# GFNet mixing and SiLU block: the last inverse stage with the tables as weights, rows r and 94 - r folded, sixteen array tiles at once

## The chip, the cores and the metric

The kernel runs on one core of a Trainium2 chip. The metric is device time in microseconds of one launch. A profiled execution also has a span, from the first to the last instruction.

## The reference, cut to what matters

Per batch of 3008 tokens and 256 channels a real Fourier transform over the tokens is multiplied by a filter and transformed back. The result goes, as 24064 tokens, through a two-layer block with SiLU.

```python
X = np.fft.rfft(x, axis=1)                   # x: (8, 3008, 256)
F = (filt_r + 1j * filt_i)[None, :, :]
y = np.fft.irfft(X * F, n=3008, axis=1)
h = y.reshape(24064, 256) @ w_in             # w_in: (256, 2048)
g = h * (1.0 / (1.0 + np.exp(-h)))
out = g @ w_out                              # w_out: (2048, 256)
```

x and the filters are float32; w_in and w_out arrive as float64, and the kernel turns their bits into float32 at its start.

## The kernel before

**The dense block sets the beat.** It runs in 384 steps. A step takes one pair of token blocks (256 or 240 columns) and one pair of 128-wide pieces of the 2048 hidden channels, by a Strassen-like scheme: seven products in `hidden` (line L957, banks px and pyz), and seven in `project` (L1020, four banks acc, a0 to a3) for the step before. ScalarE copies px to abc and applies SiLU, VectorE adds the pyz halves and combines g (L928). A float32 product is two matmul records. A step has eight rounds: in each, `hidden` advances by one product, then `project` by one. In a step in `opened`, two products of `project` come first and none in rounds 0 and 2. In a step in `joined` the first products of a new pair go to banks a0 and a1 before a2.

**The transform is put in between.** 48 steps (six pairs) belong to one batch; I call them a frame and number them 0 to 47. While the steps of batch b run, the transform of batch b + 1 is finished and that of b + 2 begun. `put(step, round, piece, ...)` says after which round of which step a piece is issued; `at = 48 * b`, so `at - 10` is step 38 of the frame before. The engines' queues are in order: a piece waits for what is issued ahead of it. The pieces for batches 2 to 7, with their steps in a frame:

- `reverse_x` (16) copies x with its rows reversed to DRAM (xr); `load_fold` (23, 33, 41) brings x and xr to x_all, 8 DMAs on SP; `fold` (28 to 30, 36 to 38, 44 to 46) adds and subtracts them on VectorE (L499); `stage1_fold` (32, 40, 0) is the first forward stage (L509): 16 products of 24 rows, 32 columns and 512 moving columns, one in each 32x32 tile of the array; `evict_fold` (ScalarE) and `pairs_fold` (VectorE, stores by POOL) empty its banks.
- `load_x`, `sums`, `stage1` (1 to 4) do the two leftover columns of the first stage.
- `load_t2`, `forward_two` (8, 16, 24), `free_two`, `multiply_two`, `add_two` (9 to 12 for the first) do the second forward stage and the filter.
- `inverse_two` (16, 24, 32), `even_two`, `rows_two`, `ends_two` do the first inverse stage and write d2 in DRAM.
- `load_t4`, `stage3` and `evict_y` are the last inverse stage, in eight groups of four positions. A group is 32 products (L742): the data (48 rows by 64 channels) are the weights, a table of 47 columns is the moving operand, channels come out on partitions. Its two banks are copied to y (L764), one by VectorE and one by ScalarE, 376 columns each. The groups stand in steps 37/38 (0 and 1, alone at the opening), 40 (2 and 3), 0 (4), 8 (5) and 11/12 (6 and 7); in the last frame in 0, 8, 11 and 16.

Batch 0 is transformed ahead of the first step, which begins at 75.25 us, in its own way (four of its last groups stand in steps 10 to 18), and batch 1 with other forward pieces; its last stage stands like that of the others.

`tokens` forms the sums ty of a pair on VectorE (L928), at (6,1), (11,5), (22,5), (26,6), (38,1) and (46,1), given as step and round. Stores of the result and all loads above are issued by SP. A wait at the head of its queue holds what is behind.

PSUM has eight banks: px and pyz (called HIDDEN), a0 to a3 (ACCS are a2 and a3) and two spare ones. A piece's `home` says which it takes; a bank of HIDDEN must be empty again before the next step's products.

Of the kernel before, what the change touches and what calls it, by code (L numbers as in the profile page):

```python
# [79 lines left out]

def rows_of(blocks):

    out = np.empty((B, NR, 2, 16, 4, 2, 32), np.float32)
    for (b, half, c0, n), block in zip(token_pairs(), blocks):
        for k in range(4):
            r0 = (c0 + n * (k // 2)) // 16
            out[b, r0:r0 + n // 16, half, :, :, OUT_HALF[k]] = (
                block[k, :, 0:n].reshape(4, 32, n // 16, 16).transpose(2, 3, 0, 1))
    return out.reshape(B * S, C)
# [100 lines left out]
def folded_tables():  # L190
# [14 lines left out]
    wn = np.zeros((128, 2, N1))  # L205
    for g in range(NG):
        for bank in range(2):
            for j in range(4):
# [7 lines left out]
                if j % 2 == 0:  # L216
                    row = 16 * (g // 2) + 4 * j + 4 * (g % 2) + 2 * bank
                    for h in range(2):
                        ph = 2 * np.pi * ((2 * np.arange(N1) + h) * s % 94) / 94
                        for half in range(2):  # L220
                            wn[64 * h + row, half] = 2 * np.cos(ph) / S if s else 1.0 / S
                            wn[64 * h + row + 1, half] = (2 * half - 1) * 2 * np.sin(ph) / S if s else 0.0
    f32 = np.float32
    return d.reshape(128, NS * 32).astype(f32), e.reshape(128, NG * 128).astype(f32), wn.astype(f32)
# [3 lines left out]
def kernel(  # L228
# [24 lines left out]
    dn_host, en_host, wn_host = folded_tables()  # L253
    dn_dram = nc.inline_tensor(dn_host, name="dn_tbl")
    en_dram = nc.inline_tensor(en_host, name="en_tbl")
    wn_dram = nc.inline_tensor(wn_host, name="wn_tbl")
# [28 lines left out]
    wn_t = cpool.tile([128, 2, N1], FP32)  # L285
# [29 lines left out]
    y = {}  # L315
# [18 lines left out]
    def spectral(b):  # L334
# [151 lines left out]
        def fold(f, k):  # L486

            used = slice(0, 120)
            if k == 0:
                us["f"] = upool.tile([128, 2, 512], FP32, name=f"uf_{b}_{f}", tag="u")  # L490
# [10 lines left out]
        def stage1_fold(f):  # L501
            ut = us.pop("f")
            rhs = x_all[:, 0, 0], x_all[:, 1, 0], ut[:, 0], ut[:, 1]
            home = (*HIDDEN, *ACCS) if f == 0 else (0, 1, None, None)
# [200 lines left out]
        def rows(g, i, n=1):  # L705
# [6 lines left out]
            for a in range(n):  # L712
                a0 = 8 * (g + a) + 4 * i
                nc.gpsimd.dma_start(out=d2[a0:a0 + 4].rearrange("a n h c -> (a n) h c"), in_=qt[:, a])
# [13 lines left out]
        def stage3(g, home=None):  # L728

            half, n0 = divmod(4 * g, 16)  # L730
            back = b > 1 and half
            table = wn_t[:, half] if b > 1 else wi_t
# [3 lines left out]
            t4 = us["t4"][:, 4 * g:4 * g + 4] if b == 0 and g < 4 else t4s[g]  # L736
            for cb in range(2):
                for i in range(4):
                    for c0 in (0, 64):
                        for h in range(2):  # L740
                            rows = slice(64 * h, 64 * h + 2 * NS)
                            nc.tensor.matmul(  # L742
                                out=ps[h][c0:c0 + 64, cb, 3 - i if back else i, :],
                                lhsT=t4[rows, i, 128 * cb + c0:128 * cb + c0 + 64],
                                rhs=table[rows, :], start=True, stop=True)
            if g < 6 and (b > 0 or g > 3):
# [11 lines left out]
        def evict_y(g, h):  # L758
            half, n0 = divmod(4 * g, 16)
            if b > 1 and half:  # L760
                n0 = 12 - n0
# [3 lines left out]

        return dict(us=us, store_rows=store_rows, evict_y=evict_y, pairs_t1=pairs_t1, halves=halves, load_first=load_first, stage1_first=stage1_first, fill_first=fill_first, load_x=load_x, load_two=load_two, sums=sums, stage1=stage1, reverse_x=reverse_x,
                    load_fold=load_fold, fold=fold, stage1_fold=stage1_fold, evict_fold=evict_fold, pairs_fold=pairs_fold, forward_two=forward_two, free_two=free_two, multiply_two=multiply_two, add_two=add_two, inverse_two=inverse_two, even_two=even_two, rows_two=rows_two, ends_two=ends_two,
                    load_t2=load_t2, forward=forward, multiply=multiply, add=add, inverse=inverse, inverse_first=inverse_first, rows_first=rows_first, even=even, rows=rows, load_t4=load_t4, load_t4_rows=load_t4_rows, stage3=stage3)
# [12 lines left out]
    def plan(b, part):  # L781
# [6 lines left out]
        else:  # L788
            put(at - 80, 0, part["reverse_x"])
            for f, step, load, places, ends in (  # L790
                    (0, -64, -73, ((-68, 3), (-68, 5), (-67, 5), (-66, 5)), ((1, 0), (1, 3))),
                    (1, -56, -63, ((-60, 3), (-60, 5), (-59, 5), (-58, 5)), ((1, 3), (1, 5))),
                    (2, -48, -55, ((-52, 3), (-52, 5), (-51, 5), (-50, 5)), ((1, 3), (1, 5)))):
# [7 lines left out]
            opened.add(at - 63)  # L801
# [30 lines left out]
        put(at - 14, 5, part["load_t4"], 0)  # L832
        put(at - 14, 5, part["load_t4"], 1)
        open_step(at - 10, *alone(part, 0), (part["stage3"], 1))
        put(at - 10, 3, part["evict_y"], 1, 0)
        put(at - 10, 5, part["evict_y"], 1, 1)
        join(at - 8, part, 2, 3)
# [12 lines left out]
    def plan_two(b, part):  # L850
# [18 lines left out]
        put(at - 12, 1, part["load_t4"], 0)  # L869
        put(at - 12, 1, part["load_t4"], 1)  # L870
        two_alone(at - 10, part, 0)
        join(at - 8, part, 2, 3)
        plan_rest(b, part)

    def two_alone(step, part, g):

        open_step(step, *alone(part, g), (part["stage3"], g + 1))
        put(step, 3, part["evict_y"], g + 1, 0)
        put(step, 5, part["evict_y"], g + 1, 1)
# [25 lines left out]
    def plan_rest(b, part):  # L905
# [6 lines left out]
        else:  # L912
            join(at, part, 4)
            join(at + 8, part, 5)
            if b == B - 1:
                alone_at(at + 11, 3, part, 6)
                join(at + 16, part, 7)
            else:
                two_alone(at + 12, part, 6)
# [178 lines left out]
    def load_weights(j, queue=None):  # L1098
# [4 lines left out]
        else:  # L1103
# [18 lines left out]
            in_=moe_w_in.bitcast(U32)[:, 256 * j:256 * j + 256].rearrange("(a p) n -> p a n", p=128))  # L1122
# [322 lines left out]
```

## Time and profile before

| | before |
|---|---|
| device time, median of 3 runs | 2573.54 us (2571.95 to 2575.02) |
| profiled execution, device time | 2574.01 us |
| its span | 2571.5 us |
| granted TensorE clock, mean | 0.996 |
| last stage's matmuls (L742, batches 2 to 7): busy, records | 52.8 us, 3072 |
| its weight loads | 48.5 us, 3072 |
| its copies to y (L764): VectorE, ScalarE | 32.9 us x60, 28.5 us x60 |
| first fold stage's matmuls (L509), two rows | 21.3 + 20.3 us, 576 |
| waits of pyz for VectorE's g (PEld, PE) | 27.7 us, 10.5 us |

Ends of matmuls are modelled and the matmuls are pipelined, so that a busy share of TensorE is not its share of the peak. A row of a group reads: line, engine, operation, out<-in, shapes, count, then busy us and mean ns of one, then the engine's idle time before it with what ended it. A row of the timeline reads: start us, us, engine, line, operation, out<-in, count, and in brackets the idle time before it.

### The profile page before, as it was taken

Reading aid. Unit: us, or ns where it says so; the run is one execution under the profiler, and the core shown is the slowest. Engines: PE = TensorE matmul, PEld = TensorE weight load, DVE = VectorE, ACT = ScalarE, POOL = GpSimd, SP = SyncE. Lnnn points to the kernel's source line nnn. Section 1 sums busy time; section 2 is a strip of 40 time slices with the busy share of each in tenths; the row PEclk is TensorE's granted clock in tenths of the full one; section 3 lists DMA queues with packets and bytes.
Section 4 is the critical chain, followed back from the end, with each engine's and each line's share of the span. In section 5 each row is a group of like instructions: output and inputs, shape, how many; then the busy total and the mean of one; then the engine's idle time right before and its main releaser. Section 6 shows DMA issues by size and latency. Waiting matters only on the chain.

```text
span 2571.5 us, 47151 instructions
## 1 busy us (share of the span) xinstructions
PE 2531.8 (98%) x18810; PEld 2183.9 (85%) x18810; DVE 1660.8 (65%) x3451; ACT 1103.6 (43%) x3039; POOL 438.5 (17%) x682
## 2 busy tenths in 40 slices
PE   8999999999999999999999999999999999999998
PEld 6688788888888888888888888888888888888987
DVE  7866656577666776667766676666766666554544
ACT  3544344444444444444444444444444444444443
POOL 3211111022111111211121111211121111101101
PEclk9999999999999999999999999999999999999999
DMA  9622142222322222331324203332042211200000
GB/s 288 163 69 78 39 111 59 65 62 65 72 68 69 58 69 59 85 83 35 75 55 97 72 25 75 83 78 63 25 98 61 60 42 33 62 15 16 16 9 17
DMA packets 122740, 171.84 MB, mean 67 GB/s; under 512 B 20500, under 2 KB 96244, under 8 KB 121636
## 3 DMA queue, kind: packets, MB, share of 16 engines
q1 hardware_dynamic: 97352, 117.88, 18.0%
q0 software_dynamic: 22320, 45.80, 6.7%
q10 hardware_dynamic: 2848, 5.15, 0.7%
q8 instruction: 147, 2.41, 0.4%
q14 instruction: 73, 0.60, 0.1%
HBM read 96.91 MB, written 81.26 MB: 69 GB/s over the span
## 4 chain that ended last, share of the span: by engine, by line
PE 93%; DVE 3%; DMA 3%; ACT 1%; issue 0%; SPq 0%; ACTq 0%; POOL 0%; POOLq 0%; DVEq 0%
PE acc L1020 43%; PE px L957 25%; PE pyz L957 19%; PE pd L742 3%; PE pc L604 1%; PE pb L566 1%; DVE g L928 1%; PE pf L509 1%; DVE q L616 1%; PE pa L420 0%; DMA filt<-in_filt_i_dram 0%; DMA w_t<-in_x_dram 0%; DMA d<-q 0%; DMA w_t<-d 0%; DVE ty L928 0%
## 5 line engine op out<-in xcount | busy, mean ns | idle before, releaser
L1020 PE MATMUL acc<-g,w_t 128*128 128x256 f32 (+1 forms) x5376 | 1509.2, 375 | 2.8 <-DVE tf L445 2.4
L1020 PEld LDWEIGHTS acc<-g,w_t 128*128 128x128 f32 x5376 | 1020.6, 190 | 128.0 <-ACT q L610 9.5
L928 DVE TENSOR_TENSOR g<-pyz,abc 128x256 f32<-128x256 f32 (+1 forms) x1152 | 479.4, 416 | 612.0 <-ACT abc L978 335.9
L928 DVE TENSOR_TENSOR g<-g 128x256 f32<-128x256 f32 (+3 forms) x1152 | 592.9, 515 | 196.7 <-ACT g L961 183.6
L957 PE MATMUL px<-ty,w_t 128*128 128x256 f32 (+1 forms) x2304 | 678.0, 376 | 1.1 <-ACT abc L972 0.6
L961 ACT ACTIVATE g<-g 128x256 f32<-128x256 f32 (+1 forms) x1152 | 473.0, 411 | 259.2 <-DVE g L928 258.9
L928 POOL TENSOR_TENSOR s<-s 128x256 f32<-128x256 f32 (+1 forms) x331 | 256.1, 791 | 1654.5 <-DVE s L1038 1434.9
L957 PEld LDWEIGHTS px<-ty,w_t 128*128 128x128 f32 x2304 | 434.1, 190 | 59.9 <-ACT abc L972 3.9
L957 PE MATMUL pyz<-y,w_t 128*128 128x256 f32 (+1 forms) x1536 | 456.1, 379 | 10.9 <-DVE g L928 10.3
L957 PEld LDWEIGHTS pyz<-y,w_t 128*128 128x128 f32 x1536 | 282.0, 190 | 65.1 <-DVE g L928 26.6
L972 ACT COPY abc<-px 128x256 f32<-128x256 f32 (+1 forms) x384 | 141.3, 368 | 367.3 <-PE px L957 367.3
L978 ACT COPY abc<-px 128x256 f32<-128x256 f32 (+1 forms) x384 | 141.5, 369 | 319.3 <-PE px L957 319.1
L961 ACT ACTIVATE g<-px 128x256 f32<-128x256 f32 (+1 forms) x384 | 145.8, 380 | 298.4 <-PE px L957 298.4
L957 PE MATMUL px<-y,w_t 128*128 128x256 f32 (+1 forms) x768 | 231.3, 383 | 0.7 <-DVE y L756 0.7
L957 PE MATMUL pyz<-ty,w_t 128*128 128x256 f32 (+1 forms) x768 | 225.8, 376 | 0.2 <-DVE g L928 0.2
L957 PEld LDWEIGHTS px<-y,w_t 128*128 128x128 f32 x768 | 142.1, 190 | 25.4 <-ACT t L427 4.9
L957 PEld LDWEIGHTS pyz<-ty,w_t 128*128 128x128 f32 x768 | 143.3, 190 | 20.2 <-DVE g L928 1.0
L965 ACT COPY abc<-px 128x256 f32<-128x256 f32 (+1 forms) x384 | 135.2, 352 | 53.7 <-PE px L957 53.7
L1038 ACT COPY s<-acc 128x512 f32<-128x512 f32 (+1 forms) x94 | 54.2, 577 | 47.6 <-issue 28.5
L742 PEld LDWEIGHTS pd<-wn_t,t 48*64 48x64 f32 x3072 | 48.5, 135 | 16.6 <-ACT g L961 11.7
L625 POOL DMA_DIRECT2D d<-low x36 | 22.2, 618 | 194.0 <-DVE low L621 194.0
L742 PE MATMUL pd<-wn_t,t 48*64 48x47 f32 x3072 | 52.8, 232 | 1.2 <-issue 1.0
(157 smaller groups left out, 1346.8 us busy)
## 6 DMA issues: line engine op xcount, KB each, us to landing
t<-d SPq DMA_DIRECT2D x120, 192.0 KB
t<-d SPq DMA_DIRECT2D x84, 256.0 KB
out_dram<-s SPq DMA_DIRECT2D x64, 256.0 KB
d<-q POOLq DMA_DIRECT2D x48, 256.0 KB, 5.2
d<-low POOLq DMA_DIRECT2D x36, 256.0 KB, 4.2
xr<-in_x_dram SPq DMA_DIRECT2D x6, 1472.0 KB
out_dram<-s SPq DMA_DIRECT2D x30, 240.0 KB
x_all<-in_x_dram SPq DMA_DIRECT2D x72, 96.0 KB
```

Source lines behind the costliest of these rows:

```text
L509: nc.tensor.matmul(out=ps[q][32 * k:32 * k + 32], lhsT=wq_t[rows, k], rhs=rhs[k][rows], start=True, stop=True)
L566: nc.tensor.matmul(out=ps[k, ri][32 * j:32 * j + 32, a, :], lhsT=dn_t[rows, 4 * (g + a) + at, :], rhs=t2s[g + a][rows, at, :], start=True, ...
L604: nc.tensor.matmul(out=ps[j][cols, ri, :], lhsT=en_t[rows, g + a, k, ri, :], rhs=zs[k, ri][0][rows, a, :], start=True, stop=True)
L742: nc.tensor.matmul(out=ps[h][c0:c0 + 64, cb, 3 - i if back else i, :], lhsT=t4[rows, i, 128 * cb + c0:128 * cb + c0 + 64], rhs=table[rows, ...
L928: eng.tensor_tensor(out=out, in0=in0, in1=in1, op=op)
L957: nc.tensor.matmul(out=out, lhsT=w_t[:, jp, c, 0], rhs=rhs, start=start, stop=True, skip_group_check=True)
L961: nc.scalar.activation(out=g[:, k, 0:n], in_=g[:, k, 0:n] if src is None else src, func=AFT.Silu)
L965: nc.scalar.copy(out=sums[:, 0, 0:n], in_=xo)
L972: nc.scalar.copy(out=sums[:, 1, 0:n], in_=xo)
L978: nc.scalar.copy(out=sums[:, 2, 0:n], in_=xo)
L1020: nc.tensor.matmul(out=acc[pair][i][:, h, 0:n], lhsT=w_t[:, jp, c, 1], rhs=g[:, k, 0:n], start=(jp == 0 and h == 0), stop=last, skip_group ...
L1038: copy(out=s[:, 2 * i:2 * i + 2, 0:n], in_=acc[pair][i][:, :, 0:n])
```

## The change

For batches 1 to 7 the last inverse stage is turned round. The table wm (24 output rows of cosines or sines by residue) becomes the weights, and the data (24 rows, 8 positions of 64 channels, 512 columns) the moving operand. A `stage3_wide` does eight positions: 16 products, one in each 32x32 tile, into four banks: for both parities of the row, the part that is even and the part that is odd under r to 94 - r. Channels stand in the columns then. `turn_wide` has VectorE transpose each bank in 32x32 squares to SBUF (one of the four by way of a ScalarE copy, `copy_wide`). `fold_wide` adds even and odd parts to rows r and subtracts them to rows 94 - r, into y. Tokens stand in another order (`token_order`, undone on the host), and channels 2p and 2p + 1 share a partition p, so the rows of w_in are split by pairs, and batch 0's stage3 reads every second column as weights. `load_wide` brings d2 in 8 DMAs on SP, of pieces of 512 bytes; `load_t4` had 2 for half as many positions.

The four `stage3_wide` of a batch stand in step 38 (opened, alone), 40 and 0 (joined, each ahead of a stage1_fold), and 6 (opened, alone). Steps 8, 11, 12 and 16 have no last stage any more. stage1_fold takes px, pyz, a3 and a spare bank in steps 40 and 0, and its second pairs_fold comes 0.75 step later; the fold in step 38 goes to 37. For batches 3 to 7 the first fold moves from steps 28 to 30 to steps 10 to 12 of the same frame, its loads to step 5 and reverse_x to step 4, and its sums stand in a buffer of t4 until step 32.

```diff
+def fold_rows(h):
+
+    return [2 * ((i + 1) % 24) if h == 0 else 2 * i + 1 for i in range(24)]
...
-    wn = np.zeros((128, 2, N1))
+    wm = np.zeros((128, 32))
...
-                    row = 16 * (g // 2) + 4 * j + 4 * (g % 2) + 2 * bank
+                    row = 8 * (g // 2) + 2 * j + 2 * (g % 2) + bank
                     for h in range(2):
-                        ph = 2 * np.pi * ((2 * np.arange(N1) + h) * s % 94) / 94
-                        for half in range(2):
-                            wn[64 * h + row, half] = 2 * np.cos(ph) / S if s else 1.0 / S
-                            wn[64 * h + row + 1, half] = (2 * half - 1) * 2 * np.sin(ph) / S if s else 0.0
+                        ph = 2 * np.pi * (np.array(fold_rows(h)) * s % 94) / 94
+                        wm[64 * h + row, 0:24] = 2 * np.cos(ph) / S if s else 1.0 / S
+                        wm[64 * h + 32 + row, 0:24] = -2 * np.sin(ph) / S if s else 0.0
...
-                us["f"] = upool.tile([128, 2, 512], FP32, name=f"uf_{b}_{f}", tag="u")
+                place, tag = (t4pool, "t4") if f == 0 and b > 2 else (upool, "u")
+                us["f"] = place.tile([128, 2, 512], FP32, name=f"uf_{b}_{f}", tag=tag)
...
-            home = (*HIDDEN, *ACCS) if f == 0 else (0, 1, None, None)
+            home = (*HIDDEN, *ACCS) if f == 0 else (*HIDDEN, 3, None)
...
-                a0 = 8 * (g + a) + 4 * i
+                a0 = 16 * (g // 2) + 8 * i + 4 * a
...
-            t4 = us["t4"][:, 4 * g:4 * g + 4] if b == 0 and g < 4 else t4s[g]
+            t4 = us["t4"][:, 4 * g:4 * g + 4] if g < 4 else t4s[g]
...
-                                lhsT=t4[rows, i, 128 * cb + c0:128 * cb + c0 + 64],
-                                rhs=table[rows, :], start=True, stop=True)
-            if g < 6 and (b > 0 or g > 3):
+                                out=ps[h][c0:c0 + 64, cb, i, :],
+                                lhsT=t4[rows, i, 2 * c0 + cb:2 * c0 + 128:2],
+                                rhs=wi_t[rows, :], start=True, stop=True)
...
+        def load_wide(k):
+            t4s[k] = [t4pool.tile([128, 8, C // 2], FP32, name=f"t4_{b}_{k}_{cb}", tag="t4") for cb in range(2)]
+            for cb in range(2):
+                for r in range(4):
+                    nc.sync.dma_start(
+                        out=t4s[k][cb][32 * r:32 * r + 24],
+                        in_=d2[r % 2::2, 8 * k:8 * k + 8, r // 2, 128 * cb:128 * cb + 128])
+
+        def stage3_wide(k, home):
+
+            ps = [bank(b, f"pd_{b}_{k}_{r}", home[r]) for r in range(4)]
+            for q in range(4):
+                for r in range(4):
+                    rows = slice(32 * r, 32 * r + 24)
+                    nc.tensor.matmul(
+                        out=ps[r][32 * q:32 * q + 32].rearrange("p a c -> p (a c)").rearrange(
+                            "p (n c) -> p n c", n=8),
+                        lhsT=wm_t[rows, :], rhs=t4s[k][q // 2][rows, :, 64 * (q % 2):64 * (q % 2) + 64],
+                        start=True, stop=True)
+            if k < 3:
+                load_wide(k + 1)
+            if k % 2 == 0:
+                y[b, k // 2] = ypool.tile([128, 2, HALF], FP32, name=f"y_{b}_{k // 2}", tag="y")
+            us["pd", k] = ps
+
+        def copy_wide(k, r):
+            raw = ppool.tile([128, 2, C], FP32, name=f"p_{b}_{k}_{r}", tag="p")
+            nc.scalar.copy(out=raw, in_=us["pd", k][r])
+            us["pd", k][r] = raw
+
+        def turn_wide(k, *rs):
+            for r in rs:
+                t = zpool.tile([128, 2, C], FP32, name=f"z_{b}_{k}_{r}", tag="z").rearrange("p a c -> p (a c)")
+                nc.vector.transpose(out=t.rearrange("p (n a c) -> p n a c", n=8, a=2), in_=us["pd", k][r].rearrange("p a c -> p (a c)").rearrange(
+                    "p (n c a) -> p n a c", n=8, a=2))
+                us["turned", k, r] = t.rearrange("p (n a i) -> p a n i", n=8, i=32)
+
+        def fold_wide(k, h):
+
+            dst = y[b, k // 2].rearrange("p a (n h i) -> p a h n i", n=16, h=2)[:, :, h, 8 * (k % 2):8 * (k % 2) + 8]
+            even, odd = us.pop(("turned", k, 2 * h)), us.pop(("turned", k, 2 * h + 1))
+            for at, n, op in ((0, 24, ALU.add), (24, 23, ALU.subtract)):
+                nc.vector.tensor_tensor(out=dst[:, :, :, at:at + n], in0=even[:, :, :, 0:n], in1=odd[:, :, :, 0:n], op=op)
...
-            put(at - 80, 0, part["reverse_x"])
+            put(at - (80 if b == 2 else 92), 0, part["reverse_x"])
+            early_fold = (-73, ((-68, 3), (-68, 5), (-67, 5), (-66, 5))), (-91, ((-86, 3), (-86, 5), (-85, 5), (-84, 5)))
             for f, step, load, places, ends in (
-                    (0, -64, -73, ((-68, 3), (-68, 5), (-67, 5), (-66, 5)), ((1, 0), (1, 3))),
-                    (1, -56, -63, ((-60, 3), (-60, 5), (-59, 5), (-58, 5)), ((1, 3), (1, 5))),
-                    (2, -48, -55, ((-52, 3), (-52, 5), (-51, 5), (-50, 5)), ((1, 3), (1, 5)))):
+                    (0, -64, *early_fold[b > 2], ((1, 0), (1, 3))),
+                    (1, -56, -63, ((-60, 3), (-60, 5), (-59, 3), (-59, 5)), ((1, 3), (2, 3))),
+                    (2, -48, -55, ((-52, 3), (-52, 5), (-51, 5), (-50, 5)), ((1, 3), (2, 3)))):
...
-            opened.add(at - 63)
+                joined.add(at + step)
+                opened.add(at + step + 1)
...
-        put(at - 12, 1, part["load_t4"], 0)
-        put(at - 12, 1, part["load_t4"], 1)
-        two_alone(at - 10, part, 0)
-        join(at - 8, part, 2, 3)
         plan_rest(b, part)
...
-            join(at, part, 4)
-            join(at + 8, part, 5)
-            if b == B - 1:
-                alone_at(at + 11, 3, part, 6)
-                join(at + 16, part, 7)
-            else:
-                two_alone(at + 12, part, 6)
+            put(at - 12, 1, part["load_wide"], 0)
+            for k, step in ((0, -10), (3, 6)):
+                open_step(at + step, (part["stage3_wide"], k, (*HIDDEN, None, None)), (part["turn_wide"], k, 0),
+                          (part["copy_wide"], k, 1))
+                put(at + step, 3, part["turn_wide"], k, 2, 3)
+                put(at + step, 5, part["turn_wide"], k, 1)
+                put(at + step + 1, 3, part["fold_wide"], k, 0)
+                put(at + step + 1, 5, part["fold_wide"], k, 1)
+            for k, step in ((1, -8), (2, 0)):
+                put(at + step, 7, part["stage3_wide"], k, (0, 1, 2, None))
+                put(at + step, 7, part["turn_wide"], k, 0)
+                put(at + step, 7, part["copy_wide"], k, 1)
+                put(at + step + 1, 0, part["turn_wide"], k, 2)
+                put(at + step + 1, 5, part["turn_wide"], k, 3, 1)
+                put(at + step + 2, 5, part["fold_wide"], k, 1)
+                put(at + step + 3, 3, part["fold_wide"], k, 0)
+                joined.add(at + step)
+                opened.add(at + step + 1)
...
-            in_=moe_w_in.bitcast(U32)[:, 256 * j:256 * j + 256].rearrange("(a p) n -> p a n", p=128))
+            in_=moe_w_in.bitcast(U32)[:, 256 * j:256 * j + 256].rearrange("(p a) n -> p a n", a=2))
...
-                          (40, en_flat, en_dram), (40, wn_t, wn_dram)):
+                          (40, en_flat, en_dram), (30, wm_t, wm_dram)):
```

## The prediction

> **What bounds the kernel now.** I read the page's head and its chain of waits, then the groups of instructions by form, then the timeline. TensorE bounds it:
>
> ```profile
> span 2571.5 us, 47151 instructions
> PE 2531.8 (98%) x18810; PEld 2183.9 (85%) x18810; DVE 1660.8 (65%) x3451; ACT 1103.6 (43%) x3039; POOL 438.5 (17%) x682
> PE 93%; DVE 3%; DMA 3%; ACT 1%; issue 0%; SPq 0%; ACTq 0%; POOL 0%; POOLq 0%; DVEq 0%
> ```
>
> But the 65% of VectorE is a mean. From the timeline I take the length of each step, from one step's first L957 px<-y matmul to the next. A plain step is 6.04 us with 256 columns (5.67 with 240; 5.85 at the changes) and every batch repeats one frame of 48 steps (310.6 to 311.3 us). What a frame takes above plain steps is the transform. I call it "extra" and number steps within the frame. One place holds no added TensorE work and is still long, steps 26 and 27 (6.38 and 7.93):
>
> ```profile
> 1200.30 1.40 DVE L616 TENSOR_TENSOR q<-q,pc 128x512 f32<-128x512 f32 x2
> 1201.62 0.42 DVE L928 TENSOR_TENSOR g<-pyz,abc 128x256 f32<-128x256 f32 x1
> 1201.95 0.68 DVE L621 TENSOR_TENSOR low<-q 128x512 f32<-128x512 f32 x1
> 1202.67 0.69 DVE L622 TENSOR_TENSOR q<-q 128x512 f32<-128x512 f32 x1
> 1203.28 0.68 DVE L928 TENSOR_TENSOR ty<-y 128x512 f32<-128x512 f32 x1
> 1204.00 0.88 DVE L928 TENSOR_TENSOR ty<-y,ty 128x256 f32<-128x256 f32 x2
> 1204.80 0.42 DVE L928 TENSOR_TENSOR g<-pyz,abc 128x256 f32<-128x256 f32 x1
> 1205.27 0.70 PE L957 MATMUL pyz<-y,w_t 128*128 128x256 f32 x2 [1.62 <-DVE g L928]
> ```
>
> Each g<-pyz add frees a bank that TensorE needs. Queued behind four other operations it comes late and TensorE idles. From undisturbed steps I get VectorE's room. After a step's first px<-y, the early adds end at 2.85 us. The second pyz add must start by 5.14 (S4 waits for it). S4 starts at 5.61 and the third pyz add must start by S4 + 0.83, or the next A12 is late. So 2.29 us fit into rounds 2 and 3, and 1.6 into rounds 5 and 6. Back to back, 512-column operations start 0.60 apart, 256-column ones 0.34 to 0.40, and 1024-column folds (1225 ns) by the same overlap 1.14.
>
> **What the stage costs now.** The form rows:
>
> ```profile
> L742 PE MATMUL pd<-wn_t,t 48*64 48x47 f32 x3072 | 52.8, 232 | 1.2 <-issue 1.0 <-DVE g L928 0.3
> L509 PE MATMUL pf<-x_all,wq_t 24*32 24x512 f32 x288 | 21.3, 598 | 0.0
> L764 DVE COPY y<-pd 128x376 f32<-128x376 f32 x60 | 32.9, 548 | 27.1 <-PE pd L742 27.0
> L370 DVE STREAM_TRANSPOSE w_t<-pa 128x512 f32<-128x512 f32 x16 | 10.3, 693 | 5.7 <-PE pa L368 5.5
> ```
>
> Two groups alone (steps 11/12), and a fold followed by one group (step 0):
>
> ```profile
> 1107.38 2.08 PE L742 MATMUL pd<-wn_t,t 48*64 48x47 f32 x128
> 1108.58 0.55 DVE L764 COPY y<-pd 128x376 f32<-128x376 f32 x1 [0.33 <-PE pd L742]
> 1109.39 0.70 PE L957 MATMUL px<-y,w_t 128*128 128x256 f32 x2
> ...
> 1344.17 0.66 PE L509 MATMUL pf<-x_all,wq_t 24*32 24x512 f32 x8
> ...
> 1345.25 1.16 PE L742 MATMUL pd<-wn_t,t 48*64 48x47 f32 x64
> 1345.45 1.07 ACT L516 COPY tf<-pf 128x512 f32<-128x512 f32 x2 [0.29 <-PE pf L509]
> 1346.34 0.70 PE L957 MATMUL px<-y,w_t 128*128 128x256 f32 x2
> ```
>
> A group of 64 matmul records holds TensorE about 1.05 us; so does a fold (32 records of 24x512, 1345.25 - 1344.17 = 1.08), and its banks reach a reader 1.28 us after its start. A stage3_wide has the fold's very form, 24 rows by 32 columns by 512, sixteen places of the array. So four replace eight groups: in busy TensorE 4.3 us a batch instead of 8.4.
>
> **The change, place by place** (extra in us per full frame, before, then after).
>
> *Steps 37 to 39.* Before 9.01 + 5.28 + 6.28 - 18.12 = 2.45. After, stage3_wide(0) stands there alone: px is refilled only when turn_wide(0) has emptied it, at 1.28 + 0.69 + 0.05 = 2.02 after the start; the two groups took 1109.39 - 1107.38 = 2.01. Half of the TensorE work thus buys nothing: the wait for VectorE takes its place. Then VectorE has the ty sums (they end 3.81 after px<-y) and turns 2 and 3 in round 3 (two at 0.63, the L370 starts) before the second pyz add: it starts at 5.07, but must by 4.38, in this shortened step. A stall of 0.69 + 0.06. After: 2.96.
>
> *Steps 40/41.* Before 9.05 + 5.77 - 11.53 = 3.29. After: wide, then fold, 2.14. The reordered projection wants bank a0 first, which turn_wide(0) empties behind the 512-column g operation, at 2.3; plus 0.1 for the restart: 2.42. ScalarE's copies are in time. Gain 0.87.
>
> *Steps 0 to 2.* Before 8.12 + 6.15 - 12.08 = 2.19 with only one group. After 2.31, and in step 2 round 5 holds fold_wide (0.93: two operations of 384 and 368 columns, between L928's rows) and the sums of x (1.20): 2.13 against 1.6, so 0.52 + 0.11 restart. After: 2.94.
>
> *Step 6.* Before nothing, after stage3_wide(3) alone with the ty sums of (6,1): 2.96, as in 38.
>
> *Step 8.* Before 2.71. After forward_two alone, whose banks are not px and pyz: 1.07 + 0.1 = 1.17.
>
> *Steps 11/12.* Before 2.21, after 0.
>
> *The moved fold.* Out of 28 to 30: frame 6, where no fold follows, has 6.04 and 6.04 in steps 28 and 29 instead of 6.32 and 6.21: gain 0.45. The long step 27 is 7.93 there too, so it stays. Into 10 to 12: step 10 already holds the adds of round 3 (2 x 0.60) and two products in round 5 (1.20); the fold adds 1.14 to each. The second pyz add starts at 2.85 + 2.34 = 5.19, the third at 5.19 + 0.33 + 2.34 = 7.86, due 6.49: 1.37 + 0.11. In step 11 round 5 the ty sums (1.45) and two fold operations (1.20) are 2.65 where 1.62 fit: 1.03 + 0.11. Step 12 fits. Together 2.65, close to the 2.23 of steps 26/27 under a like load.
>
> Sum of a full frame: before 2.45 + 3.29 + 2.19 + 0 + 2.71 + 2.21 + 0.45 = 13.30; after 2.96 + 2.42 + 2.94 + 2.96 + 1.17 + 0 + 2.65 = 15.10: +1.8, five frames +9.0. Frame 0 (only 38 and 40): -0.36. Frame 6 (no new fold in 10 to 12 or 40): +0.36. Frame 7 (before 1.23 + 1.43 + 1.28 + 1.45; after 2.31 + 2.96): -0.12. In all +8.9: a span of 2580.4. The run takes 2.0 more than the span if the median 2573.54 is set against it (the profiled run itself was 2574.01), so **2582.4 us**.
>
> *At nothing.* ScalarE does four copies (589 ns) for eight (476): less. load_wide is 8 DMAs a time where two load_t4 were 4, of 512-byte pieces instead of 1024, with the same bytes. At 0.45 us an issue it costs SP 3.6 us; the packets of a load before ran 5 us, and the need comes some 10 (step 38) to 35 us later. Without that cover every late microsecond stalls TensorE. At step 1 it goes ahead of load_x (8 DMAs), 2.7 us later, with some 5 us in hand. xr is now copied from about step 2 of SP's queue; its packets ended 32 us after issue before, so near 48 us into the frame. load_fold's first read of xr waits for it, and behind that the other reads and four load_t2 queue, for forward_two at about 62: some 6 us in hand. POOL gets the same 8 stores, those of pairs_fold 0.75 step later. Tables and the split of moe_w_in by row pairs: same number of pieces.
>
> *Not in the trace.* Weights read at every second column (batch 0, 8 groups): between 0 (the strided moving operand of L548: 389 against 382 ns) and twice the 16 ns a load, 8 us; I take 0. A transpose out of SBUF: 0.59 to 0.72 apart as L370's. A wide matmul's rows of 64 strided columns: L368's 16-column pieces cost 493 ns for 384, L411's 595 for 512, one line; I take the fold's.
>
> By the Trainium skill ("Trainium Kernel Development and Optimization", Best Practices), tiling speeds up TensorE's compute but not the emptying of PSUM, which speaks against this change. The rows agree: 8 x 2 x 376 columns were emptied per batch, now 16 x 512. By the rule alone steps 40/41 would gain nothing either, and the sum would be 6 x 0.87 = 5.2 more.
>
> **Rivals.** (1) *VectorE absorbs it*: if transposes, folds and the moved fold never make a pyz add late, each full frame loses the terms 0.75 + 0.75 + 0.63 + 2.65, and frames 0, 6, 7 lose 0.75, 2.13, 0.75: 27.5 less, -18.6: 2555 us. For it: steps 18 to 20 carry four 512-column operations without a stall. Against: those are 2.4 us, step 10 has 4.7. It decides faster if over a third of that lag is missing. (2) *Half of the lag*: 2568.7, at the edge of no change. (3) *Sixteen tiles do not overlap*, so the change doesn't do what it says: at four at once a wide is 3 x 0.85 = 2.6 longer, 28 of them +71: 2655. Against it, the fold's 1.08. (4) *SP's queue*: if xr takes over 38 us beside load_wide and load_x, load_t2 is late and step 8 stalls, 5 x up to 4 = +20: 2602.
>
> **How the numbers follow.** Likeliest, lag as counted: 0.53, own range 2573 to 2594. Rival 1: 0.22; rival 2: 0.15; rival 3: 0.02; rival 4: 0.08. 0.2% (5 us) is about what a measurement of this kernel tells from none. Rival 1 and part of rival 2 are faster: 0.27; within 0.2%: 0.16; slower 0.57. The range leaves out most of rival 1 and the ends of 3 and 4: 2561 to 2597.
>
> **What would show it.** TensorE busy falls, yet steps 38 and 6 stay near 9 us. Waits of pyz on the L928 g add grow from 38 us (10.5 + 27.7) by 10 or more, with step 11 of frames 1 to 5 over 7 us. Steps 28 and 29 fall to 6.04, 27 stays 7.93, 40 loses under 1. Wrong if step 10 to 12 are plain, if a wide's px<-y comes much before 2.0 us, or if forward_two waits for a DMA.

## The result and the profile after

| | before | after |
|---|---|---|
| device time, median of 4 runs | 2572.74 us (2570.84 to 2575.02) | 2698.67 us (2697.04 to 2699.26) |
| ratio, 95% interval | | 1.0488 (1.047 to 1.0506) |
| span of the profiled execution | 2571.5 us | 2697.3 us |
| granted TensorE clock, mean | 0.996 | 0.975 |

The kernel became 126 us slower; 8.9 were forecast. Medians leave out an execution at a clearly lower clock: one of "Only xr's move" below, its profiled one, took 2744.66 us at a granted clock of 0.932 and is not in its median. The head of the page and two rows of the 40 slices show at once that this is not spread evenly. Each digit is a tenth of a slice of 67 us, first TensorE's busy share, then its granted clock:

```profile
span 2697.3 us, 42139 instructions
...
PE 2526.0 (94%) x16122; PEld 2146.4 (80%) x16122; DVE 1750.8 (65%) x3619; ACT 1099.3 (41%) x3011; POOL 438.6 (16%) x682
...
PE   8999996999969999699996999969999999999998
...
PEclk9999998999989999899998999989999999999999
```

TensorE's busy time fell from 2531.8 to 2526.0 us (to 2513.7 in the first experiment, where the hole is gone), and its share fell from 98% to 94%: it waits. Before, its row had nines everywhere but at the two ends:

```profile
PE   8999999999999999999999999999999999999998
```

Now five slices, five apart, show 6, and the clock shows 8 in the same five. Five slices are 337 us, about a frame with its hole: one hole in each of five frames. The groups of instructions say who waits (busy us and mean ns, then the engine's idle time before the group and what ended it):

```profile
L1016 PE MATMUL px<-y,w_t 128*128 128x256 f32 (+1 forms) x768 | 231.7, 384 | 117.5 <-ACT t L447 103.8
...
L447 DVE COPY t<-pa 128x512 f32<-128x512 f32 x6 | 4.2, 692 | 106.6 <-DMA d<-tf 106.3
...
L447 ACT COPY t<-pa 128x512 f32<-128x512 f32 x22 | 12.0, 585 | 111.0 <-DMA d<-tf 109.8
```

`hidden` (now L1016) stood 103.8 us behind a ScalarE copy of stage1 (L447), and that copy stood 109.8 us behind a DMA, the stores of tf. The list of waits (us, how many, the longest) gives the count, and beside it the wait on which the forecast was built:

```profile
ACT t L447 <- DMA d<-tf: 109.8, 5, 22.6
...
PEld pyz L1016 <- DVE g L987: 56.6, 74, 2.0
PE pyz L1016 <- DVE g L987: 30.1, 39, 1.6
```

Five waits of up to 22.6 us. None of them is in the kernel before, where the same copy (L427 there) waited only for its matmul:

```profile
ACT t L427 <- PE pa L420: 6.1, 6, 1.0
```

The wait of pyz on VectorE's g was 27.7 and 10.5 us before; together it went from 38 to 87, in the direction forecast.

With the steps measured as in the prediction (from one step's first px<-y to the next), after less before, summed over the frames:

| steps | forecast | after | after, xr copied earlier (first experiment) |
|---|---|---|---|
| 37 to 39 | +3.6 | +3.6 | +3.6 |
| 40 to 42 | -5.2 | -3.1 | -3.1 |
| 0 to 4 | +5.6 | **+120.6** | +5.7 |
| 5 to 7 | +20.7 | +21.3 | +21.4 |
| 8, 9 | -10.7 | -7.9 | -7.9 |
| 10 to 12 | -1.3 | -1.8 | -1.8 |
| 28, 29 | -2.2 | -2.2 | -2.2 |
| 32, 33 (frame 0) | 0 | -3.9 | -3.9 |
| 16 (frame 7) | -1.4 | -1.3 | -1.3 |
| sum | +9 | +125.3 | +10.5 |

Forecasts by place are the prediction's terms of a frame times its frames. One row is off by 115 us, in frames 1 to 5 alone: step 3 lasts 29.6 to 31.0 us there where frame 6, which copies no xr, has 9.50, and step 4 lasts 6.8 to 8.3 where frame 6 has 5.28. The other rows are off by up to 3.9 us each; their errors have both signs and leave 1.2 together. The stall forecast for round 5 of step 2 stands in the row of steps 0 to 4 too: it holds up the second product of step 3, and in "xr earlier" step 3 lasts 9.50 us instead of 8.88.

The timeline of frame 2 shows how it comes about (start us, us, engine, line, operation):

```profile
755.42 0.67 SPq L486 DMA_DIRECT2D xr<-in_x_dram  x1
756.14 1.20 SPq L490 DMA_DIRECT2D xr<-in_x_dram  x2
...
757.81 0.52 POOL L549 DMA_DIRECT2D d<-tf  x1 [7.96 <-DVE tf L465]
...
761.39 0.50 POOL L549 DMA_DIRECT2D d<-tq  x1
...
766.94 1.09 PE L440 MATMUL pa<-u,wf_t 47*64 47x512 f32 x8
...
789.08 0.59 ACT L447 COPY t<-pa 128x512 f32<-128x512 f32 x1 [22.02 <-DMA d<-tf]
789.12 0.69 DVE L447 COPY t<-pa 128x512 f32<-128x512 f32 x1 [21.34 <-DMA d<-tf]
...
789.71 1.22 PE L1016 MATMUL px<-y,w_t 128*128 128x256 f32 x2 [20.83 <-ACT t L447]
```

SP issues the copy of x with its rows reversed (xr) at 755 to 757. Two to six microseconds after the first of these issues POOL issues the eight stores of pairs_fold. tf, tq and stage1's t come from one pool of two buffers, so the copy L447 may write t only when the stores of tf have landed; px and pyz hold stage1's result until then, and TensorE stops.

The packets in the trace give the reason for the 22 us. xr's large DMA is 46 packets of 32 KB, nearly all 1.213 us long. They run from 757.0 to 788.6, so that fewer than two are under way on average (46 x 1.213 / 31.5 = 1.8; there are 16 engines). The stores are 192 packets of 4 KB (0.24 us on average). Of these, 164 had started by 763.8; the other 28 trickled until 788.8, as long as xr's packets ran.

The order of the late packets shows what held them. From 764.5 to 787.5 the trace has 36 packets of xr and 36 of POOL's queue (24 of 4 KB, 12 of 4 bytes). xr's come in two series, 0.28 us apart, and in each series exactly one packet of POOL's queue stands between two of xr's: one of xr at 769.92, a store's at 771.13, xr's at 771.29, one of 4 bytes at 772.50, xr's at 772.50, a store's at 773.71, and so on. So a late store packet, 0.159 us long, passed only after 1.2 us of another copy. In the kernel before, xr was issued at 1091.8, 46 us after the last of that frame's stores (issued from 1041.7 to 1045.7).

By the Trainium skill ("DMA: Bandwidth & Descriptors", Queues, rings and completion order), a DMA engine with work from several queues takes a packet of each in turn. The alternation above agrees: the small packets that share an engine with large ones pass at the pace of the large ones. The same page (Rules for kernel authors) says that an outermost dimension below 16 keeps a DMA on at most as many engines; that of xr is 2, and the two series agree.

### The profile page after: what moved, and what is told of

It is laid out like the page before. It is cut to its first block, busy times and chain, and to the rows that moved or that the text cites. A ratio compares the mean times of both kernels' runs of the same rounds, so it can differ in the third digit from the quotient of the medians.

```text
span 2697.3 us, 42139 instructions
## 1 busy us (share of the span) xinstructions
PE 2526.0 (94%) x16122; PEld 2146.4 (80%) x16122; DVE 1750.8 (65%) x3619; ACT 1099.3 (41%) x3011; POOL 438.6 (16%) x682
## 5 line engine op out<-in xcount | busy, mean ns | idle before, releaser
L1016 PE MATMUL px<-ty,w_t 128*128 128x256 f32 (+1 forms) x2304 | 679.0, 376 | 1.1 <-ACT abc L1031 0.6
L1016 PE MATMUL pyz<-y,w_t 128*128 128x256 f32 (+1 forms) x1536 | 461.0, 382 | 30.4 <-DVE g L987 29.9
L1016 PEld LDWEIGHTS px<-ty,w_t 128*128 128x128 f32 x2304 | 435.7, 191 | 60.6 <-ACT abc L1031 3.7
L1016 PEld LDWEIGHTS pyz<-y,w_t 128*128 128x128 f32 x1536 | 281.4, 190 | 92.9 <-DVE g L987 55.6
L1016 PE MATMUL px<-y,w_t 128*128 128x256 f32 (+1 forms) x768 | 231.7, 384 | 117.5 <-ACT t L447 103.8
L1016 PEld LDWEIGHTS px<-y,w_t 128*128 128x128 f32 x768 | 143.8, 191 | 155.3 <-ACT t L447 109.1
L1016 PE MATMUL pyz<-ty,w_t 128*128 128x256 f32 (+1 forms) x768 | 227.2, 378 | 0.2 <-DVE g L987 0.2
L1016 PEld LDWEIGHTS pyz<-ty,w_t 128*128 128x128 f32 x768 | 143.4, 191 | 21.5 <-DVE g L987 1.0
L447 DVE COPY t<-pa 128x512 f32<-128x512 f32 x6 | 4.2, 692 | 106.6 <-DMA d<-tf 106.3
L816 DVE STREAM_TRANSPOSE z<-pd 128x512 f32<-128x512 f32 x84 | 56.5, 698 | 6.3 <-PE pd L797 6.3
L447 ACT COPY t<-pa 128x512 f32<-128x512 f32 x22 | 12.0, 585 | 111.0 <-DMA d<-tf 109.8
```

What stands on the lines that cost most here:

```text
L447: copy(out=t1[:, h], in_=ps[h])
L816: nc.vector.transpose(out=t.rearrange("p (n a c) -> p n a c", n=8, a=2), in_=us["pd", k][r].rearrange("p a c -> p (a c)").rearrange("p (n ...
L1016: nc.tensor.matmul(out=out, lhsT=w_t[:, jp, c, 0], rhs=rhs, start=start, stop=True, skip_group_check=True)
```

## The experiments

Two theories of the hole stood against each other at first, and the forecast's own terms had to be tried as well. **A**: xr's packets hold up the stores on the engines that they share, so that either another time for xr or another form of its packets must remove it. **B**: the stores come too late, since pairs_fold moved by 0.75 step, and xr matters little.

**xr earlier.** reverse_x goes nine steps ahead, to step 43 of the frame before.

```diff
-            put(at - (80 if b == 2 else 92), 0, part["reverse_x"])
+            put(at - (80 if b == 2 else 101), 0, part["reverse_x"])
```

> The changed kernel with the copy of reversed x put 9 steps earlier (frame step 43 instead of 4), the early fold and all else kept. Theory A (the copy runs while the stores of tf and tq are under way and holds them up on the DMA engines that both use, so the buffer that stage1 copies to comes free some 20 us late): step 3 falls from 30 us to about 9.5 and the time to 2576 to 2588. Rival B (the second pairs_fold, 0.75 step later, is by itself too late for the two buffers of t): step 3 stays near 30 us, 2685 to 2700. What remains over before is then the sum of the other places, +7 to +9 us.

Measured: 2585.07 us (2584.09 to 2586.83), ratio to before 1.0046 (1.0031 to 1.0061). The 114 us are gone. In its timeline the same copy of frame 2 waits for its matmul alone:

```profile
743.25 1.09 PE L440 MATMUL pa<-u,wf_t 47*64 47x512 f32 x8
...
744.39 0.59 ACT L447 COPY t<-pa 128x512 f32<-128x512 f32 x1 [1.02 <-PE pa L440]
744.43 0.69 DVE L447 COPY t<-pa 128x512 f32<-128x512 f32 x1 [0.34 <-PE pa L440]
```

xr's packets (684.6 to 714.7) now run beside the stores of another fold, issued at 685.7 to 689.2. Those buffers are next written at 723.6, when ScalarE empties the next fold's banks; by then all has landed. The overlap alone costs nothing; it costs where somebody waits.

**Stores back.** The ends of the folds in steps 40 and 0 get the time that they had before.

```diff
...
-    (1, -56, -63, ((-60, 3), (-60, 5), (-59, 3), (-59, 5)), ((1, 3), (2, 3))),
-    (2, -48, -55, ((-52, 3), (-52, 5), (-51, 5), (-50, 5)), ((1, 3), (2, 3)))):
+    (1, -56, -63, ((-60, 3), (-60, 5), (-59, 3), (-59, 5)), ((1, 3), (1, 5))),
+    (2, -48, -55, ((-52, 3), (-52, 5), (-51, 5), (-50, 5)), ((1, 3), (1, 5)))):
```

> The changed kernel with the second pairs_fold of folds 1 and 2 back at round 5 of the step after, the copy of reversed x still in step 4. The stores are then issued some 5 us earlier, about when the copy's first packets start. Theory A: most of the wait goes, step 3 9 to 15 us, 2575 to 2620, with VectorE a little later in step 1. Rival B: all of the wait goes too, 2575 to 2590. If the copy alone were enough whenever the stores are issued (Rival C), step 3 stays over 25 us and the time over 2670.

Measured: 2674.75 us (2669.15 to 2681.99), ratio 1.0386 (1.0366 to 1.0407). The hole is smaller and still there: steps 3 and 4 cost 87.6 us over before, and without xr in the way they cost 3.7. The stores of frame 2 go out at 751.8 to 755.4, and xr's packets begin at 753.2. VectorE pays for it elsewhere, as steps 2 and 42 grow by 1.1 and 1.3 us each. B falls as the cause; the 0.75 step sets only how deep the hole is.

**The first fold back.** The fold of steps 10 to 12, its loads, reverse_x and its buffer return to their old places; the new last stage stays.

```diff
...
-            put(at - (80 if b == 2 else 92), 0, part["reverse_x"])
+            put(at - 80, 0, part["reverse_x"])
...
-                    (0, -64, *early_fold[b > 2], ((1, 0), (1, 3))),
+                    (0, -64, *early_fold[0], ((1, 0), (1, 3))),
```

> The changed kernel with the first fold, its loads and the copy of reversed x back at their old steps (28 to 30, 23, 16). Theory A: step 3 near 9.5 us; steps 10 to 12 plain, steps 28 and 29 long by 0.45 again: five times 2.24 us less than the run with the copy put earlier, so 2566 to 2576, about as before. Rival B: over 2670.

Measured: 2572.52 us (2572.09 to 2576.2), ratio 1.0000 (0.9991 to 1.0009). Steps 10 to 12 are plain and the hole is gone. The last stage as it is placed here is worth nothing: what steps 8 to 12 and 16 lose (24.5 us) is spent again in steps 5 to 7, 0 to 4 and 37 to 39 (30.8 us), on the wides that now stand there and on TensorE's waits for VectorE. Without the 3.8 us of steps 32 and 33 in frame 0, which are not the stage's (see below), it would cost some 3 us. Steps 28 and 29 are 6.32 and 6.21 again, so that the moved fold had saved 0.45 a frame there, as forecast.

**xr spread.** xr stays at step 4, but its copy has pieces of 2 KB with sixteen as the outermost dimension.

```diff
-            nc.sync.dma_start(out=us["xr"][:, 1:24],
-                              in_=bass.AP(tensor=x.tensor, offset=at + 46 * 32 * C,
-                                          ap=[[32 * N1 * C, 2], [-32 * C, 23], [1, 32 * C]]))
+            for k in range(2):
+                nc.sync.dma_start(out=us["xr"][k, 1:24].rearrange("m (s n) -> s m n", s=16),
+                                  in_=bass.AP(tensor=x.tensor, offset=at + (46 + N1 * k) * 32 * C,
+                                              ap=[[2 * C, 16], [-32 * C, 23], [1, 2 * C]]))
```

> The changed kernel, every step as it is, with the copy of reversed x cut into pieces of 2 KB, sixteen outermost, so that it is spread over the DMA engines (one more DMA). Theory A with few engines as the cause: the copy ends in 6 to 12 us instead of 29, the stores land with it, step 3 is 9.5 to 13 us, 2576 to 2605. If the bytes of the copy or the HBM are what hold the stores up (Rival D), spreading them does not help and step 3 stays over 20 us, 2650 to 2700.

Measured: 2585.23 us (2583.22 to 2586.21), ratio 1.0045 (1.003 to 1.006): the time of "xr earlier", with xr issued where the changed kernel has it, ahead of the same stores. In frame 2 its packets are over about 8 us after the first, instead of 31.5. A holds, and its cure is the form of the copy.

**Only xr's move, in the kernel before.** Nothing else of the change is in it.

```diff
-            put(at - 80, 0, part["reverse_x"])
+            put(at - (80 if b == 2 else 92), 0, part["reverse_x"])
```

> The kernel before with one edit: the copy of reversed x issued in frame step 4 instead of 16 for batches 3 to 7 (its loads and the fold stay in 23 and 28 to 30). Theory A (the copy on few DMA engines holds up the stores that run beside it, and stage1 waits for their buffer): the stores of fold 2 are issued at about the same time here, so step 3 grows from 8.9 us by 5 to 22 in five frames: 2595 to 2690. If something of the new last stage is needed for the wait (the later pairs_fold, load_wide on SP), step 3 stays under 10 us and the time is 2572 to 2578.

Measured: 2657.78 us (2653.76 to 2658.18), ratio 1.0321 (1.0304 to 1.0338), 83.6 us more than before. The move of one copy makes the hole without the new stage: in the profiled run step 3 lasts 18.5 to 27.1 us in frames 1 to 5 and 9.2 in frame 6. Its depth is about that of "stores back" (87.6 - 3.7 = 83.9 in its profiled run), which has the stores at the same place.

**Small packets, few engines.** The copy keeps its outer dimension of 2 and is cut into eight DMAs of 4 KB pieces. This separates the packet's size from the number of engines.

```diff
+            for s in range(8):
+                nc.sync.dma_start(out=us["xr"][:, 1:24, 4 * C * s:4 * C * s + 4 * C],
+                                  in_=bass.AP(tensor=x.tensor, offset=at + 46 * 32 * C + 4 * C * s,
+                                              ap=[[32 * N1 * C, 2], [-32 * C, 23], [1, 4 * C]]))
```

> The changed kernel, steps as they are, the copy of reversed x in eight DMAs of 4 KB pieces with the same outer dimension of two, so that it still goes over few DMA engines but in small packets. If the shared engines take packets of the two queues in turn, a stored 4 KB packet then waits for a 4 KB packet (0.2 to 0.3 us) instead of a 32 KB one (1.21 us): step 3 near 9.5 to 13 us, 2583 to 2605. If an engine finishes what is queued first, or the copy's whole time on the two engines counts, step 3 stays at 25 to 32 us, 2670 to 2705.

Measured: 2594.42 us (2590.47 to 2595.31), ratio 1.0075 (1.006 to 1.009). xr's packets run even longer than before (733.9 to 769.1, 0.16 us each), and step 3 lasts 9.5 to 10.0 us. In frame 2 the last of the same stores starts at 745.0, 10 us after the first issue, and its packets stand between those of xr in the same way: the stores pass between small packets. So few engines alone do not make the hole; the packets must be large too. Large packets spread over many engines were not tried. Of the 9 us over "xr spread" some 6 lie in step 8 (8.4 to 9.2 us in frames 1 to 5 instead of 7.56), and SP's queue in frame 2 shows why:

```profile
732.44 17.54 SPq L487 DMA_DIRECT2D xr<-in_x_dram  x8
...
755.66 0.48 SPq L501 DMA_DIRECT2D x_all<-in_x_dram  x1
769.88 0.31 SPq L504 DMA_DIRECT2D x_all<-xr  x1
...
772.99 9.97 SPq L556 DMA_DIRECT2D t<-d  x8
```

load_fold's first read of xr stands at the head of the queue from 756 to 769.9, until xr has landed, 37 us after its first issue. Behind it load_t2 (L556), which forward_two of step 8 needs, goes out at 773.0; in "xr spread" it went at 761.6. This is the prediction's fourth rival, seen in small.

**The moved fold, three steps later.** From here on the spread copy is in every version of the changed kernel. The fold goes to steps 13 to 15, where VectorE has nothing else of the transform.

```diff
...
-  (-91, ((-86, 3), (-86, 5), (-85, 5), (-84, 5)))
+  (-91, ((-83, 3), (-83, 5), (-82, 5), (-81, 5)))
```

> The changed kernel with the copy spread and the first fold in steps 13 to 15 instead of 10 to 12. By the late pyz adds of step 10 and 11: steps 10 to 12 and 13 to 15 plain (6.04), 5 x 2.7 less than 2585: 2569 to 2574. By total load: the stall moves along, 2580 to 2586.

Measured: 2571.01 us (2569.45 to 2574.71), ratio 0.999 (0.9981 to 0.9999): 14.2 less than "xr spread", and steps 10 to 15 are plain.

**The ty sums out of the steps with a wide alone.**

```diff
...
-    combines = ((-2, 1), (6, 1), (11, 5), (22, 5), (26, 6), (38, 1))
+    combines = ((-2, 1), (5, 1), (11, 5), (22, 5), (26, 6), (35, 5))
```

> The changed kernel with the copy spread and the ty sums out of the two steps in which a stage3_wide stands alone: (6,1) to (5,1), (38,1) to (35,5). By the second pyz add late behind the ty sums and two transposes: steps 38 and 6 get 0.75 shorter, thirteen times, 2573 to 2578. If the 3.0 us of these places are all the wait for px, nothing changes: 2584 to 2587.

Measured: 2573.89 us (2571.68 to 2574.69), ratio 0.9998 (0.9988 to 1.0007): 11.3 less than "xr spread". Steps 38 and 6 are 5.28 instead of 6.03 and 6.09, in fourteen places (the expectation counted thirteen), 10.9 us in all.

**All of these together**, and the sums of step 26 moved to (31,1).

```diff
...
-    combines = ((-2, 1), (6, 1), (11, 5), (22, 5), (26, 6), (38, 1))
+    combines = ((-2, 1), (5, 1), (11, 5), (22, 5), (31, 1), (35, 5))
```

> The changed kernel with the copy of reversed x spread over the DMA engines, the first fold in steps 13 to 15 and three of the ty sums moved: (6,1) to (5,1), (38,1) to (35,5), (26,6) to (31,1). If late pyz adds are what the other places cost: 2585 less 5 x 2.69 (steps 10 to 12), 13 x 0.75 (steps 38 and 6) and 6 x 1.9 (steps 26 and 27), 2547 to 2558, faster than before by 0.6 to 1%. If VectorE is late for its total of work and not for where the work stands, the stalls come back in the new places, 2570 to 2585.

Measured: 2550.63 us (2549.12 to 2551.01), ratio 0.9909 (0.9894 to 0.9924), the fastest of all. Its head and its waits:

```profile
PE 2506.8 (98%) x16122; PEld 2142.8 (84%) x16122; DVE 1753.6 (69%) x3619; ACT 1096.0 (43%) x3011; POOL 437.5 (17%) x682
```

```profile
PEld pyz L1017 <- DVE g L988: 19.4, 44, 1.0
...
PE pyz L1017 <- DVE g L988: 3.0, 8, 0.6
```

VectorE does as much as in the changed kernel (1753.6 us to 1750.8), and the waits on its g are 22 us instead of 87 (87 in "xr earlier" too, which has no hole either). Only the places differ.

**One move in the kernel before.** What of that gain needs no new stage?

```diff
-    combines = ((-2, 1), (6, 1), (11, 5), (22, 5), (26, 6), (38, 1))
+    combines = ((-2, 1), (6, 1), (11, 5), (22, 5), (31, 1), (38, 1))
```

> The kernel before with one edit: the ty sums of (26,6) at (31,1). By the late pyz add of steps 26 and 27: step 27 loses most of its 1.9 us, six times, 2560 to 2565, and the rest of the 23 us by which the version with all moves beats the kernel before is the new last stage. If it were the total load of VectorE in 26 to 28, step 27 stays over 7 us, 2571 to 2576.

Measured: 2564.49 us (2560.42 to 2565.76), ratio 0.996 (0.9946 to 0.9974), with step 27 at 6.41 instead of 7.93. So some 10 of the 23.6 us are this move alone. Of the other 14, by the steps, 2.2 come from the fold's move out of steps 28 and 29 and 3.9 from steps 32 and 33 of frame 0; about 8 are left for the new stage with its pieces in better places. Neither of these two gains was tried by itself in the kernel before. The three moves add up: 14.2 + 11.3 + 9.6 = 35.1 from 2585.23 gives 2550.1, and 2550.63 was measured.

## Why the prediction was right and wrong

**Wrong: a copy at nothing.** The step that failed stands under "At nothing": "xr is now copied from about step 2 of SP's queue; its packets ended 32 us after issue before ... some 6 us in hand", and "POOL gets the same 8 stores, those of pairs_fold 0.75 step later". I followed the moved copy through SP's queue and to its reader and never asked what else would be on the DMA engines in those 32 us. It should have been a term of the sum. The trace of before held it: xr's packets run 28 us (1095.8 to 1123.8 there), and from the first of the stores to the copy that needs their buffer pass 13.7 us (1041.7 to 1055.4), or 10 with the stores at their later place (734.1 to 744.4 in "xr earlier"). Hence up to 18 us a frame, 90 in all, if the stores are held to the end; 114 were measured, deeper since xr's packets last 31.5 us in company and TensorE starts again at half pace. The range, 2561 to 2597, could not hold what no term held.

**Right: the rest.** Without the hole the changed kernel takes 2585.1 to 2585.2 us, by two different cures; 2582.4 were forecast. That it comes so close is partly luck: steps 40 to 42 and 8, 9 gained 4.9 us less than forecast, and steps 32 and 33 of frame 0 gained 3.9 that nothing forecast. The direction, and the reason that the forecast gave for it, stand: the matmuls are halved and VectorE takes the gain back. Three views of after show it in the terms of the forecast. First the form rows of the new stage, which answer to L742 and L764 of before (31.9 us for seven batches, 4.6 a batch, where 52.8 for six were 8.8):

```profile
L797 PE MATMUL pd<-t,wm_t 24*32 24x512 f32 x896 | 31.9, 600 | 0.0
...
L816 DVE STREAM_TRANSPOSE z<-pd 128x512 f32<-128x512 f32 x84 | 56.5, 698 | 6.3 <-PE pd L797 6.3
```

A wide's 16 tiles overlap as the fold's do (in frame 2 the fold behind a wide starts at 745.62, 0.88 after the wide at 744.74), so rival 3 falls. Then step 38 of frame 2, whose wide stands alone:

```profile
1012.33 1.14 PE L797 MATMUL pd<-t,wm_t 24*32 24x512 f32 x32
...
1013.63 0.72 DVE L816 STREAM_TRANSPOSE z<-pd 128x512 f32<-128x512 f32 x1 [0.46 <-PE pd L797]
...
1014.40 0.70 PE L1016 MATMUL px<-y,w_t 128*128 128x256 f32 x2 [0.93 <-DVE z L816]
...
1018.23 1.31 DVE L816 STREAM_TRANSPOSE z<-pd 128x512 f32<-128x512 f32 x2
...
1019.46 0.39 DVE L987 TENSOR_TENSOR g<-pyz,abc 128x256 f32<-128x256 f32 x1
...
1019.89 0.70 PE L1016 MATMUL pyz<-y,w_t 128*128 128x256 f32 x2 [0.48 <-DVE g L987]
```

px<-y starts 2.07 us after the wide (forecast 2.02), when the first transpose has emptied px. The second pyz add starts 5.06 after that (forecast 5.07), behind the ty sums and two transposes, and TensorE stands for it. "The ty sums out" takes away this stall: 11.3 us in time, 10.9 in the fourteen steps (14 x 0.75 = 10.5 by the forecast's term). Last, step 11 with the moved fold:

```profile
838.16 1.22 DVE L520 TENSOR_TENSOR x_all<-x_all 120x1024 f32<-120x1024 f32 x1
839.29 0.42 DVE L987 TENSOR_TENSOR g<-pyz,abc 128x256 f32<-128x256 f32 x1
...
839.76 0.70 PE L1016 MATMUL pyz<-y,w_t 128*128 128x256 f32 x2 [1.11 <-DVE g L987]
```

The add is queued behind a fold operation of 1.22 us, and TensorE idles 1.11. Steps 10 to 12 cost 2.69 us a frame (forecast 2.65). "Three steps later" gives back 14.2 us in time, 13.4 in its steps (forecast 13.3). With this rival 1, that VectorE absorbs the work, and rival 2, half of the lag, fall: the waits are as large as counted. (Rival 3's price was added up wrongly: 2582.4 + 71 is 2653, not 2655.)

**Terms of a wrong size.** Steps 40 to 42 gained 0.44 us a frame where 0.87 were forecast: the wide and fold pair cost 2.85, not 2.42. Projection starts about when counted, but the rest of the two steps was taken as plain. Step 8 costs 1.63, not 1.17: forward_two holds TensorE for 1.43 us, from its first matmul to the next px<-y (at 1091.36 and 1092.79 in "xr earlier"), where I had taken a group's 1.07. Step 32 of frame 0 became 3.3 us shorter (13.54 to 10.20), and step 33 0.5; nothing was forecast there. Before, TensorE waited 2.41 us for the pairs of a fold in it (L445, at 310.45). The change also puts this step in `joined`, the line `joined.add(at + step)` of its diff, so that `project` begins with banks a0 and a1, and after it that wait is gone (acc at 308.22, with no idle time before). It is no part of the new stage, and no experiment was made on it.

**Rival 4**, SP's queue, did not come in the changed kernel (step 8 is 7.56 in every frame but the first and the last); "small packets" shows what it would have been.

**What stays open.** The trace doesn't name the engine of a packet; that large and small packets shared one follows from their alternation and from the two cures. How the loss after the hole (step 4) divides is also not tried.

## What to carry to other kernels

Treat a moved copy as a load on the DMA engines and not only as an entry in a queue: list what else is in flight while its packets run, and for each of those who waits for it, buffers that a store must release among them. Give a copy in DRAM an outermost dimension of 16 and small pieces: here it was over in 8 us instead of 31.5, and nothing stood behind it long. And price work on an engine with idle time by the room in the very round where it is put: 1754 us of work on VectorE cost TensorE 22 us of waits in the fastest kernel, and 1751 us of it cost 87 in "xr earlier", where the same work lies in front of the adds that TensorE waits for.

## What was not expected of the hardware

**Few large packets of one queue stall the small packets of another.** The eight stores, 0.75 MB in 192 packets, normally land within some 3 us each. With two 32 KB packets in flight beside them, one in seven (28 of 192) had yet to start 8 us after the first issue, and the last started 31 us after it; the copy that needed the buffer began 0.1 us after the end of that last packet (788.96 and 789.08).

**TensorE starts again at half pace.** After the 20.8 us of idle time of frame 2 the pairs of matmuls follow each other 0.67 to 1.02 us apart:

```profile
789.71 1.22 PE L1016 MATMUL px<-y,w_t 128*128 128x256 f32 x2 [20.83 <-ACT t L447]
790.73 1.06 PE L1016 MATMUL pyz<-y,w_t 128*128 128x256 f32 x2
791.58 1.06 PE L1079 MATMUL acc<-g,w_t 128*128 128x256 f32 x2
792.43 0.83 PE L1016 MATMUL px<-ty,w_t 128*128 128x256 f32 x2
793.10 0.59 PE L1016 MATMUL pyz<-ty,w_t 128*128 128x256 f32 x2
```

In an undisturbed step they are 0.43 apart (755.00, 755.43, 755.87 and so on in the same frame). At 793.10, 3.4 us on, a pair lasts its usual 0.59 again and the next follows after 0.43. Step 4 lasted 1.5 to 3.0 us longer in the five frames, 10.4 in all. The granted clock of the trace tells the same: it is 0.50 from 772.4 to 792.9 in this frame, and its mean is 0.975 against 0.994 to 0.997 in the profiled runs without the hole. By the Trainium skill ("TensorE: Matmul & The Clock Gate", Part 1: The HAM clock gate) an idle window of some 3.4 us halves TensorE's clock, and about as long a busy one restores it; the rows agree (TensorE's last product before ended at 768.9, 3.5 us before the clock fell, and the clock rose 3.2 us after the restart).
